# A third q/k operand set, first weights merged in PSUM, and a planner that picks one of two engines, in an LSH attention and feed-forward kernel

## The chip, the cores and the metric

The kernel runs on one core of a Trainium2 chip. The time is the device time of one execution in microseconds (us); the profile names the engines PE (TensorE matmul), PEld (its weight loads), DVE (VectorE), ACT (ScalarE), POOL (GpSimd) and SP (SyncE, which here only issues DMAs).

## What is computed

Attention in which a query sees only the keys of its own hash bucket, then two feed-forward layers one after the other, each with its own weights. All of it in float32 or better (the feed-forward weights come as float64).

```python
def _attn_ref(q, k, v, proj):            # (2, 8, 768, 64), proj (64, 6)
    q_bits = (q @ proj > 0); k_bits = (k @ proj > 0)
    mask = bucket(q_bits)[..., :, None] == bucket(k_bits)[..., None, :]
    scores = where(mask, q @ k.T / sqrt(D), -1e9)
    attn = exp(scores - max(scores)); attn /= sum(attn) + 1e-9
    return attn @ v
...
x = attn_out as (1536, 512)              # heads side by side
h = x @ w_in1;  x = (h * sigmoid(h)) @ w_out1      # w: 512x2048, 2048x512
h = x @ w_in2;  x = (h - tanh(h)) @ w_out2
```

## The kernel before

**Precision.** TensorE multiplies in a reduced float32 form, so every operand is split into a high part (a cast) and a low part (the value minus the cast), and a product is three matmuls: high by high, high by low, low by high. The casts and subtractions are most of the element-wise work.

**Attention.** There are 16 heads (8 of each batch) with 6 tiles of 128 queries by 768 keys. For a head, q and k come by DMA into a raw tile `r`; `q_hi` and `k_hi` (casts, ACT), `q_lo` and `k_lo` (subtractions, POOL; on DVE for head 0) make four operand tiles. `hash_mm` (L369) multiplies them with the projection, DVE turns signs into bits (L389 into `hb` and by DMA into the operands; L379 and L382 directly, for head 0). These bits make the scores of unlike buckets very small. A tile then goes: scores on PE (L503, four matmuls), the softmax read with the row maximum on DVE (L507), bias and exponent on ACT (L511, L514). After that a tile takes one of two ways. A *turned* tile (`direct`; every second one of batch 0, none of batch 1) is transposed by PE in two halves (L528), split into fp16 halves by ACT (L537) and DVE (L541). Any other is split by ACT (L556, `soft_hi`) and POOL (L559, `soft_lo`) and transposed by a DMA (L562) that SP issues. Both end in 18 small matmuls with V (L577 to L579). V is split too: row maxima (L422), a scale (L429 to L439), `v_hi` on ACT (L454), `v_lo` on DVE (L458). At a head's end DVE divides (L591 to L599); for every two heads PE transposes into x (L611), which is split into `xh` and `xl` (L616, L619).

**Feed-forward.** It works in groups of twelve matmuls of 128x384 (L828 for the hidden layer, L884 for the output), 256 groups in three passes: layer 1 of batch 0 (64 groups), layer 1 of batch 1 (64), layer 2 of both (128). Pass 0 needs x of batch 0 and fills TensorE between the tiles of batch 1; pass 1 needs x of batch 1. After a group of the hidden layer ACT takes a tanh (L832), DVE gates (L838 or L840), ACT casts (L843), DVE subtracts (L846).

**Weights.** They come as float64 words, in pieces of 128x512: absolute value (ACT, L755), clip (DVE, L758), shift (DVE, L762), sign (DVE, L766), merge with the low word (DVE, L770), cast (ACT, L774), subtraction (POOL, L778). The first eight pieces (`early`) keep the intermediate in the SBUF tile `wa`, later ones in a PSUM bank `cv`. The raw piece has two buffers, `wa` has two.

**Order.** A planner (`Plan.order`, L71 to L154) sets every engine's order when the program is built: each step has one engine, an estimated cost, a key (a due time, from `KNOBS`), what it depends on and which buffer slots it takes. Engine by engine it looks at the steps that could start, takes among those within `slack` of the earliest start the one with the smallest key, and books its buffers. On the chip each engine runs its own list strictly in order. Operand tiles of q and k have two sets of their own; for the first six heads the weight tiles `h0`, `l0` serve as a third. Raw q/k tiles have one slot and, for batch 0, two borrowed from `h1` and `l1`.

## Time and profile before

| | |
|---|---|
| median of 3 runs | 778.18 us (776.93 to 781.0) |
| profiled execution | 781.89 us |
| its span | 780.1 us |
| PE busy | 727.0 us (93%) |
| DVE busy | 561.7 us (72%) |
| ACT busy | 438.8 us (56%) |
| POOL busy | 309.6 us (40%) |

The span is the time from the first to the last instruction. The shares are means over quite different parts: until about 164 us the core does attention of batch 0 alone, until about 358 us attention of batch 1 with feed-forward groups between, and from there feed-forward alone, so the profile has to be read part by part. "PEclk" is TensorE's granted clock as a share of 2.4 GHz (0.5 is 1.2 GHz). Records of one engine overlap slightly, since an instruction's record begins before the end of the one ahead; where steps follow closely, the distance of their starts is what one costs.

### The profile page before, as it was taken

What the parts mean: (1) busy time and instruction counts of PE and PEld (TensorE: products, weight loads), DVE (VectorE), ACT (ScalarE), POOL (GpSimd) and SP (SyncE); (2) the same over time, 40 slices, a digit from 0 to 9 for tenths busy, and PEclk for the clock granted to TensorE, in tenths of its full rate; (3) what the DMA queues carried; (4) which work ended last, traced back from release to release, by engine and by line L of the source; (5) the groups of instructions that cost most, each with busy time, mean ns of one, the idle gap of its engine ahead of it and who ended that gap; (6) DMA issues with size and microseconds to landing.
All of it is one profiled execution on the core that took longest, in us unless ns stands there. A gap on an engine that the chain in (4) does not pass through costs nothing.

```text
span 780.1 us, 14311 instructions
## 1 busy us (share of the span) xinstructions
PE 727.0 (93%) x5492; PEld 700.2 (90%) x5492; DVE 561.7 (72%) x1029; ACT 438.8 (56%) x821; POOL 309.6 (40%) x214
## 2 busy tenths in 40 slices
PE   3679966789999998999999999999999999999998
PEld 1559855689899998999999999999999999999998
DVE  6888999788688987887735288998688467243342
ACT  3598987789589787776535244562533235022130
POOL 4166676447676777566644322211220022000000
PEclk9899989799999999999999999999999999999999
DMA  9576675659999999895234233324032020000102
GB/s 333 191 160 157 149 168 147 171 129 225 220 215 213 260 260 197 188 211 149 69 107 108 82 109 108 109 82 134 27 110 81 1 86 24 1 1 0 58 25 82
DMA packets 138879, 100.39 MB, mean 129 GB/s; under 512 B 115870, under 2 KB 118174, under 8 KB 138810
## 3 DMA queue, kind: packets, MB, share of 16 engines
q1 hardware_dynamic: 138522, 99.20, 50.7%
q8 instruction: 43, 0.70, 0.4%
q10 hardware_dynamic: 288, 0.28, 0.2%
q14 instruction: 26, 0.21, 0.1%
HBM read 57.95 MB, written 11.53 MB: 89 GB/s over the span
## 4 chain that ended last, share of the span: by engine, by line
PE 79%; DVE 7%; DMA 5%; ACT 4%; POOL 2%; issue 2%; SPq 0%; POOLq 0%; DVEq 0%; ACTq 0%
PE psm L884 34%; PE psm L828 33%; PE ps L503 6%; DMA pt<-hl 3%; PE pso L577 1%; ACT p L514 1%; PE pso L579 1%; PE pso L578 1%; DVE p L507 1%; PE psm L369 1%; DVE wa L766 1%; POOL hl L559 1%; ACT p L537 1%; PE psm L528 1%; POOL k L351 1%
## 5 line engine op out<-in xcount | busy, mean ns | idle before, releaser
L828 PE MATMUL psm<-xh,wh 128*128 128x384 f32 x512 | 173.0, 338 | 0.2 <-ACT x L626 0.2
L828 PE MATMUL psm<-xh,wl 128*128 128x384 f32 x512 | 172.3, 337 | 0.0
L828 PE MATMUL psm<-xl,wh 128*128 128x384 f32 x512 | 172.3, 337 | 0.0
L884 PE MATMUL psm<-gh,wh 128*128 128x384 f32 x512 | 171.9, 336 | 0.0
L884 PE MATMUL psm<-gh,wl 128*128 128x384 f32 x512 | 171.4, 335 | 0.0
L884 PE MATMUL psm<-gl,wh 128*128 128x384 f32 x512 | 171.3, 335 | 0.0
L559 POOL TENSOR_TENSOR hl<-p,hl 128x768 f16<-128x768 f32 x72 | 120.3, 1672 | 113.9 <-ACT hl L556 92.5
L778 POOL TENSOR_TENSOR wl<-wa,wh 128x512 fp32r<-128x512 f32 x64 | 83.0, 1303 | 178.6 <-ACT wh L774 156.9
L832 ACT ACTIVATE th<-psm 128x384 f32<-128x384 f32 x128 | 62.9, 491 | 108.4 <-PE psm L828 108.2
L507 DVE TENSOR_SCALAR_CACHE_REDUCE p<-ps 128x768 f32<-128x768 f32 x96 | 91.0, 953 | 17.3 <-PE ps L503 15.8
L891 DVE TENSOR_TENSOR acc<-acc,psm 128x384 f32<-128x384 f32 x96 | 52.7, 551 | 67.8 <-PE psm L884 67.3
L846 DVE TENSOR_TENSOR gl<-psm,gh 128x384 fp32r<-128x384 f32 x128 | 71.2, 556 | 36.3 <-ACT gh L843 36.1
L828 PEld LDWEIGHTS psm<-xh,wh 128*128 128x128 f32 x512 | 96.1, 188 | 0.5 <-ACT x L626 0.5
L884 PEld LDWEIGHTS psm<-gh,wh 128*128 128x128 f32 x512 | 96.4, 188 | 0.0
L884 PEld LDWEIGHTS psm<-gl,wh 128*128 128x128 f32 x512 | 96.4, 188 | 0.0
L884 PEld LDWEIGHTS psm<-gh,wl 128*128 128x128 f32 x512 | 96.2, 188 | 0.0
L828 PEld LDWEIGHTS psm<-xl,wh 128*128 128x128 f32 x512 | 96.2, 188 | 0.0
L828 PEld LDWEIGHTS psm<-xh,wl 128*128 128x128 f32 x512 | 96.1, 188 | 0.0
L503 PE MATMUL ps<-k,q 128*128 128x384 f32 x336 | 84.0, 379 | 11.6 <-DVE p L507 10.1
L514 ACT ACTIVATE p<-p,bi 128x768 f32<-128x768 f32 x96 | 89.6, 936 | 4.1
L843 ACT CAST gh<-psm 128x384 fp32r<-128x384 f32 x128 | 61.3, 479 | 48.4 <-DVE psm L840 35.5
L503 PEld LDWEIGHTS ps<-k,q 128*128 128x128 f32 x336 | 62.0, 208 | 15.8 <-DVE p L507 8.6
(95 smaller groups left out, 1241.7 us busy)
## 6 DMA issues: line engine op xcount, KB each, us to landing
w<-in_w_in_dram SPq DMA_DIRECT2D x32, 512.0 KB
w<-in_w_out_dram SPq DMA_DIRECT2D x32, 512.0 KB
r<-in_qkT_dram SPq DMA_DIRECT2D x15, 768.0 KB
wi<-wa SPq DMA_DIRECT2D x16, 256.0 KB
wo<-wa SPq DMA_DIRECT2D x16, 256.0 KB
w<-wi SPq DMA_DIRECT2D x16, 256.0 KB
w<-wo SPq DMA_DIRECT2D x16, 256.0 KB
vr<-in_v_dram SPq DMA_DIRECT2D x6, 512.0 KB
```

Of the source, the lines that this page charges most:

```text
L351: eng.tensor_tensor(k1, get(raw)[:, 1, :], k2.bitcast(F32), op=ALU.subtract)
L503: nc.tensor.matmul(out=get(ps)[:, u, 0:HS], lhsT=x[:, t * 128:(t + 1) * 128], rhs=c[:, u * HS:(u + 1) * HS], start=(j == 0), stop=(j == 1))
L507: nc.vector.tensor_scalar(get_p().rearrange("p (c s) -> p c s", c=2), get(ps)[:, :, 0:HS], FLOOR, None, op0=ALU.max, op1=ALU.max, accum_ou ...
L514: nc.scalar.activation(out=get_p(), in_=get_p(), func=ACTF.Exp, scale=0.125, bias=get(bi))
L559: nc.gpsimd.tensor_tensor(get_hl()[:, 1, :], get_p(), get_hl()[:, 0, :], op=ALU.subtract)
L778: nc.gpsimd.tensor_tensor(ll, get(wa).bitcast(F32), hh.bitcast(F32), op=ALU.subtract)
L828: nc.tensor.matmul(out=ps, lhsT=a[:, k, fs], rhs=b_[blk][:, k, :], start=(k == 0 and j == 0), stop=(k == KD - 1 and j == 2))
L832: nc.scalar.activation(out=get(th), in_=get(bk)[:, 0:NB], func=ACTF.Tanh, scale=0.5 if e == 0 else 1.0)
L843: nc.scalar.copy(g_tile(gh, "gh")[:, f, :], get(bk)[:, 0:NB])
L846: nc.vector.tensor_tensor(g_tile(gl, "gl")[:, f, :], get(bk)[:, 0:NB], g_tile(gh, "gh")[:, f, :].bitcast(F32), op=ALU.subtract)
L884: nc.tensor.matmul(out=ps, lhsT=a[:, f, ds], rhs=b_.tile[:, f, :], start=(f == 0 and j == 0), stop=(f == F - 1 and j == 2))
L891: nc.vector.tensor_tensor(acc_tile(), acc_tile(), get(bk)[:, 0:NB], op=ALU.add)
```

## The change

- *Operands.* `qk_slots` gets three sets of its own; the weight tiles `h0`, `l0` no longer serve as operands (`xsets=0`), and the raw slots borrowed from `h1`, `l1` serve five heads instead of eight. The freed SBUF comes from a smaller DMA scratch buffer.
- *Weights.* Absolute value and clip now work in `wa` for all pieces, and the clip may go to POOL. The shift writes from `wa` into a PSUM bank, borrowed from the matmul banks for the first eight pieces (`banks`) and `cv` for the others; sign works in the bank, and the merge reads it and writes `wa`.
- *Two engines.* Some steps (`q_hi`, `soft_hi`, the bias, the clip, the casts of x and of the gate among them) are given several engines. The planner lists such a step under each; one that isn't the first may take it only if start, cost and a bias `b_...` come out no later than on the first engine with what is queued there. A bias of 100 leaves the first engine alone.
- *Turned tiles.* The share is 0.4 in batch 0 (19 instead of 24) and 0.083 in batch 1 (4 instead of none).
- *Order.* Scores, softmax reads, fp16 halves, transposes and products with V are each taken in the order of the tiles (`line`). New keys: head 0 and the constants come first, V and the first weights later. Head 0's q and k are loaded ahead of head 1's. Two groups of the first hidden layer may run three quarters of their matmuls before the last quarter of x is there (`ahead`).

```diff
-KNOBS = dict(start=8.965, step=2.575, gap=10.136, step1=4.004, ffn=3.742, ffn3=2.182, pv=9, prep=14.527, hash=6.75,
-             slack=0.157, conv=22.093, conv0=74.277, vld=2.059, vmax=-3.882, vsplit=1.453, x2=0)
+KNOBS = dict(start=1.134, step=2.53, gap=9.343, step1=3.92, ffn=3.61, ffn3=2.222, pv=12.257, prep=16.11, hash=8.464,
...
+        def finish(t, e, at):
+            queue = sum(x.ways[e][0] for x in pend[e] if x is not t and x.key < t.key and len(x.ways) == 1)
+            return max(at, free[e] + queue) + t.ways[e][0]
+
...
+                    start = max(at, free[e])
+                    first = next(iter(t.ways))
+                    if e != first and start + t.ways[e][0] + t.bias > finish(t, first, at):
+                        continue
...
     qk_slots = [Slot(lambda i=i: tuple(qkp.tile([128, S], F32R, tag=f"{x}{i}", name=x) for x in ("q1", "q2", "k1", "k2")))
-                for i in range(2)]
+                for i in range(3)]
...
-        raw = Held(*(one(r_slots) + (r_extra if n < H else [])))
-        ops = Held(*(one(qk_slots) + ([(wtile["h0"], wtile["l0"])] if n < 6 else [])))
+        raw = Held(*(one(r_slots) + (r_extra if n < K["raws"] else [])))
+        ops = Held(*(one(qk_slots) + ([(wtile["h0"], wtile["l0"])] if n < K["xsets"] else [])))
...
-            direct = b == 0 and i % 2 == 1
+            share = K["direct"] if b == 0 else K["direct1"]
+            direct = int((i + 1) * share) > int(i * share)
...
-                th = add("ACT", 0.83, soft_hi, a + 1.5, [e], takes=[hl], uses=[p])
-                tl = add("POOL", 1.66, soft_lo, a + 2, [th], uses=[p, hl])
-                ready = [add("SP", 1.43, flip, a + 3, [tl], takes=[pt], uses=[hl], tail=1.5)]
+                th = add(("ACT", "POOL", "DVE"), (0.83, 1.66, 0.6), soft_hi, a + K["k_hi"], [e], takes=[hl], uses=[p], port=("DVE",), give="shi", line="hl")
+                tl = add(("POOL", "DVE"), (1.66, 0.95), soft_lo, a + K["k_lo"], [th], uses=[p, hl], port=("DVE",), give="slo")
+                ready = [add("SP", 1.43, flip, a + K["k_f"], [tl], takes=[pt], uses=[hl], tail=2.25, line="pt")]
...
-                        cvh = None if early else Held(*cvs)
...
+                        cvh = Held(*(banks if early else cvs))
...
+                            a = add("ACT", 0.65, c_abs, kj, [ld], takes=[wa], uses=[w])
+                            a = add(("POOL", "DVE"), (1.29, 0.42), c_clip, kj + 0.5, [a], uses=[wa], port=("DVE",), give="clip")
+                            a = add("DVE", 0.6, c_shift, kj + 1, [a] + gate_cv, takes=[cvh], uses=[wa])
+                            a = add("DVE", 0.69, c_sign, kj + 1.05, [a], uses=[cvh, w])
+                            a = add("DVE", 0.69, c_low, kj + 1.1, [a], uses=[cvh, w, wa])
...
-                        hm = add("PE", 2.08, h_mm, tk, wdone + xready[blk], takes=[bk], uses=[held])
+                        if ps_i == 0 and c == 0 and q * F + f < K["ahead"]:
+                            xr = xready[blk]
+                            hm = add("PE", 1.56, lambda h_mm=h_mm: h_mm(0, KD - 1), tk - K["by"], wdone + xr[:-2],
+                                     takes=[bk], uses=[held])
+                            hm = add("PE", 0.52, lambda h_mm=h_mm: h_mm(KD - 1, KD), tk, [hm] + xr[-2:], uses=[bk, held])
```

Three places show how the order moves. First DVE at the start of the program, before: `wa` is a weight piece, `vm` V's row maxima, `hb` the bits of head 1.

```order
L334 CAST q_176<-r 128x768
L343 TENSOR_TENSOR q_177<-r,q_176 128x768
L422 TENSOR_REDUCE vm<-vr 128x1 x2
L389 TENSOR_SCALAR hb<-psm,cst_sb 82x384 x2
L758 TENSOR_SCALAR wa<-wa 128x512
L762 TENSOR_SCALAR wa<-wa 128x512
L766 SCALAR_TENSOR_TENSOR wa<-w,wa 128x512
L770 SCALAR_TENSOR_TENSOR wa<-w,wa 128x512
L351 TENSOR_TENSOR k_178<-r,k_179 128x768
```

And now (L334, L385 and L392 are head 0's cast and subtractions, L424 and L427 its bits, L558 the softmax read):

```order
L334 CAST q_172<-r 128x768
L385 TENSOR_TENSOR q_173<-r,q_172 128x768
L392 TENSOR_TENSOR k_174<-r,k_175 128x768
L424 TENSOR_SCALAR q_173<-psm,cst_sb 18x384
L427 TENSOR_SCALAR k_175<-psm,cst_sb 18x384
L424 TENSOR_SCALAR q_173<-psm,cst_sb 18x384
L427 TENSOR_SCALAR k_175<-psm,cst_sb 18x384
L466 TENSOR_REDUCE vm<-vr 128x1
L558 TENSOR_SCALAR p,mx<-ps 128x768 x2
L434 TENSOR_SCALAR hb<-psm,cst_sb 82x384
```

Head 0's subtraction of k, which stood behind two V steps, head 1's bits and a whole weight piece, follows its other two steps at once, and two softmax reads stand where the weight piece stood; before, the first softmax read is row 33 of the list.

Second, DVE in the middle of batch 0 at one of the first weight pieces. Before, a piece is four steps in `wa`, as in the rows above. Now (L820 clip, L823 shift, L827 sign, L831 merge; `psm` is a borrowed bank):

```order
L820 TENSOR_SCALAR wa<-wa 128x512
L558 TENSOR_SCALAR p,mx<-ps 128x768
L823 TENSOR_SCALAR psm<-wa 128x512
L645 TENSOR_SCALAR den<-pso,vsc 128x6
L646 RECIPROCAL den<-den 128x6
L827 SCALAR_TENSOR_TENSOR psm<-w,psm 128x512
L595 TENSOR_TENSOR p<-psm,p 128x384
L831 SCALAR_TENSOR_TENSOR wa<-w,psm 128x512
```

The intermediate lies in the bank from the shift to the merge, and softmax and division steps stand between.

Third, PE where feed-forward work begins. Before (L503 scores, L611 transposes of x, L828 the hidden layer):

```order
L503 MATMUL ps<-k_2015,q_2013 128x384 x2
L503 MATMUL ps<-k_2016,q_2014 128x384 x2
L611 MATMUL psm<-cst_sb,xt 128x128 x6
L503 MATMUL ps<-k_2015,q_2013 128x384 x2
L503 MATMUL ps<-k_2016,q_2014 128x384 x2
L828 MATMUL psm<-xh_78,wh 128x384
L828 MATMUL psm<-xl_80,wh 128x384
L828 MATMUL psm<-xh_78,wl 128x384
```

Now (L554 scores, L892 the hidden layer; nine such rows stand here before a transpose of a turned tile follows):

```order
L554 MATMUL ps<-k_1377,q_1375 128x384 x2
L554 MATMUL ps<-k_1378,q_1376 128x384 x2
L892 MATMUL psm<-xh_78,wh 128x384
L892 MATMUL psm<-xl_80,wh 128x384
L892 MATMUL psm<-xh_78,wl 128x384
L892 MATMUL psm<-xh_78,wh 128x384
```

Before, the first hidden group stands behind the last transposes of x of batch 0; now nine matmuls of the first group, and two transposes of tiles later nine of the second, stand among the last head's tiles, ahead of those transposes of x.

## Rows read from the trace of the kernel before

**Rows 1.** Busy time by stretch: engine sums (instructions), granted clock, DMA share, GB/s.

```profile
core 0: us, PE busy (x) PEld busy (x) DVE busy (x) ACT busy (x) POOL busy (x), PEclk, DMA share, GB/s
0.00:31.00 31.00, 11.90 (x34) 8.48 (x34) 24.28 (x40) 10.80 (x15) 8.57 (x10) 0.99 0.84 300
31.00:90.00 59.00, 52.70 (x632) 46.20 (x633) 50.89 (x112) 52.63 (x102) 35.65 (x21) 0.95 0.65 143
90.00:164.40 74.40, 54.51 (x658) 47.04 (x657) 66.25 (x123) 60.73 (x113) 44.89 (x30) 0.89 0.67 166
164.40:357.60 193.20, 188.67 (x1763) 179.63 (x1762) 161.86 (x309) 154.42 (x277) 127.40 (x82) 0.99 0.99 215
357.60:780.00 422.40, 419.16 (x2411) 418.84 (x2409) 258.44 (x447) 160.19 (x317) 93.14 (x73) 1.00 0.22 68
```

**Rows 2.** Chain that ended last (start, us, what): the first feed-forward groups.

```profile
164.36 6.36 PE psm L828 x36
```

**Rows 3.** Waits of PE from 31 to 164 us: total, times, longest.

```profile
PE ps L503 <- DVE p L507: 12.1, 9, 5.0
```

**Rows 4.** Instructions in order of time (start, us, engine, line), start of the program.

```profile
5.88 0.38 DVE L303 CAST hw<-x 128x410 fp32r<-128x410 f32 x1 [5.01 <-DMA x<-in_proj_dram]
7.24 2.02 DVE L334 CAST q<-r 128x768 fp32r<-128x768 f32 x1 [0.36 <-DMA r<-in_qkT_dram]
9.30 2.44 DVE L343 TENSOR_TENSOR q<-r,q 128x768 fp32r<-128x768 f32 x1
...
17.32 0.95 DVE L351 TENSOR_TENSOR k<-r,k 128x768 fp32r<-128x768 f32 x1
...
21.68 1.63 PE L503 MATMUL ps<-k,q 128*128 128x384 f32 x4
23.10 0.52 PE L369 MATMUL psm<-q,hw 128*82 128x384 f32 x1
...
28.26 0.61 DVE L382 TENSOR_SCALAR k<-psm,cst_sb 18x384 fp32r<-18x384 f32 x1
...
31.02 0.96 DVE L507 TENSOR_SCALAR_CACHE_REDUCE p<-ps 128x768 f32<-128x768 f32 x1
```

**Rows 5.** Groups by line and form, whole span: busy us, mean ns, idle before.

```profile
L758 DVE TENSOR_SCALAR cv<-cv 128x512 f32<-128x512 f32 x56 | 38.9, 694 | 6.5 <-ACT cv L755 6.4
L762 DVE TENSOR_SCALAR cv<-cv 128x512 int32<-128x512 int32 x56 | 38.9, 694 | 0.8
L766 DVE SCALAR_TENSOR_TENSOR cv<-w,cv 128x512 int32<-128x512 int32 x56 | 38.7, 691 | 0.7
...
L766 DVE SCALAR_TENSOR_TENSOR wa<-w,wa 128x512 int32<-128x512 int32 x8 | 9.5, 1184 | 0.2
L770 DVE SCALAR_TENSOR_TENSOR wa<-w,wa 128x512 int32<-128x512 int32 x8 | 8.2, 1019 | 0.2
L758 DVE TENSOR_SCALAR wa<-wa 128x512 f32<-128x512 f32 x8 | 5.9, 735 | 0.0
L762 DVE TENSOR_SCALAR wa<-wa 128x512 int32<-128x512 int32 x8 | 4.1, 517 | 0.2
```

**Rows 6.** Instructions in order of time: transposes, halves, and the first gating step.

```profile
85.22 0.87 PE L528 MATMUL psm<-cst_sb,p 128*128 128x128 f32 x6
...
112.86 1.01 DVE L541 TENSOR_TENSOR p<-psm,p 128x384 f16<-128x384 f32 x2
...
164.78 2.73 DVE L458 SCALAR_TENSOR_TENSOR v16l<-vr,vsc,v 128x512 f16<-128x512 f32 x4
167.45 0.56 DVE L838 SCALAR_TENSOR_TENSOR psm<-th,psm 128x384 f32<-128x384 f32 x1
```

**Rows 7.** Instructions in order of time, POOL and DVE, around a first weight piece.

```profile
105.03 1.64 POOL L559 TENSOR_TENSOR hl<-p,hl 128x768 f16<-128x768 f32 x1 [0.75 <-DVE wa L762]
105.06 2.16 DVE L766 SCALAR_TENSOR_TENSOR wa<-w,wa 128x512 int32<-128x512 int32 x1
...
122.99 1.28 POOL L778 TENSOR_TENSOR wl<-wa,wh 128x512 fp32r<-128x512 f32 x1 [3.29 <-ACT wh L774]
```

**Rows 8.** Waits of SP's queue from 31 to 164 us: total, times, longest.

```profile
SPq L562 <- POOL hl L559: 41.1, 15, 5.5
...
SPq L731 <- DVE wa L770: 2.9, 1, 2.9
```

More of the change, by code (lines that the diff above doesn't have):

```diff
@@ L353, in lsh_attention_moe_kernel @@
[L353 to L358 removed]
+            ENG[e].tensor_tensor(q2[lo, :], get(raw)[lo, 0, :], q1[lo, :].bitcast(F32), op=ALU.subtract)
```

314 lines of the change are left out of this document (179 added, 135 removed).

## The prediction

> **What bounds the kernel now.** I read the stretches first [rows 1]. From 357.6 us to the end TensorE is busy 419.2 of 422.4 us at full clock; what is missing is the last output on its way to memory. Nothing that the change does on other engines can shorten that stretch. From 164.4 to 357.6 us it is busy 188.7 of 193.2 us: attention of batch 1 with feed-forward groups between (twelve matmuls of 128x384, 2.1 us each, [rows 2]), which could as well stand later at the same rate. So the time is the moment at which feed-forward work begins to fill TensorE (164.4 us, [rows 2]), plus a nearly fixed amount of TensorE work, plus the tail. Before that moment TensorE has 119.1 us of work in 164.4, in part at half clock (granted 0.95 and 0.89 on average, [rows 1]); its longest wait there is for VectorE's softmax reads, L507, 12.1 us [rows 3]. VectorE is busy 24.3 + 50.9 + 66.3 = 141.4 us of it. ScalarE is close behind: 52.6 of 59 us between 31 and 90 [rows 1].
>
> Two things inside that first part are dear. The first softmax read starts only at 31.0 us [rows 4]: head 0's data is ordered behind head 1's, and two weight pieces and the whole V preparation stand ahead of it on VectorE, whose cast and subtraction of head 0 take 2.0 and 2.4 us while GpSimd works on another head; the next subtraction of that size (L351) takes 0.95. And the first eight weight pieces, whose intermediate lies in SBUF (wa), pay 1.18 us for the sign step L766 and 1.02 for the merge L770, where the later ones, in PSUM (cv), pay 0.69 [rows 5].
>
> **Anchor.** The profiled execution took 781.9 us (span 780.1). The median of the runs, 778.2, is 3.7 lower; I work out a difference on the profiled span and subtract it from 778.2. My mark is the first gating step L838 at 167.45 us [rows 6], since the order shows which VectorE instructions stand ahead of it in both kernels.
>
> **The change, term by term, on VectorE up to the mark.** Busy before: 141.4 plus the four V splits between (2.7, [rows 6]) = 144.1; idle so 23.3.
> - Sign step in a borrowed bank: 8 x (1.184 - 0.691) = -3.9. Merge: 8 x 1.019 = 8.2 becomes 7 x 0.69 = 4.8 (the eighth stands behind the mark): -3.4 [rows 5].
> - Clip: nine (8 x 0.735 + 0.69 = 6.6) become three (2.2), five go to GpSimd: -4.4 [rows 5].
> - Shift, now from SBUF into PSUM, a form that is not in the trace: the nearest rows are 0.517 (SBUF) and 0.694 (PSUM) [rows 5]; I take the dearer, 8 x 0.694 against 8 x 0.517 + 0.69: +0.7 (from -0.7 to +0.7).
> - Fewer turned tiles: 19 instead of 24 in batch 0, and one of batch 1 ahead of the mark, so 40 steps L541 instead of 48; two in a row take 1.01 us [rows 6]: 8 x 0.505 = -4.0.
> - Head 0 with no other head's subtraction on GpSimd beside it: at most 2.02 + 2.44 - 0.6 - 0.95 = -2.9, at least 0; I take -2.5, nearest to the 0.95 row [rows 4].
> - V splits 10 to 7: 3 x 0.7 = -2.1, merely later. Three more batch-1 softmax reads at 0.95, of which 0.07 overlaps: +2.6. One cast to fp16 moved onto VectorE: +0.6, an estimate from the shift rows.
>
> Sum: -3.9 - 3.4 - 4.4 + 0.7 - 4.0 - 2.5 - 2.1 + 2.6 + 0.6 = -16.4, so 127.7 us.
>
> **When the stage starts.** The first data still comes at 5.9 us [rows 4]. Casting the constants (0.95), then cast and two subtractions of head 0 (0.6 + 0.95 + 0.95) lead to 9.4; from the first hash matmul to the end of the last bit step 5.8 (23.10 to 28.87), first scores 1.6: the first softmax read stands at about 16.8 instead of 31.0 [rows 4]. That is no gain of 14.2 us by itself, since the V and weight work that stood there is done later. Of the 127.7 us, 6.6 lie ahead of 16.8; 121.1 follow. From 31 to 164.4 VectorE was busy 117.1 of 133.4 us, 0.878. At the same density 121.1 / 0.878 = 137.9, and the mark falls at 154.7: **12.8 us earlier**.
>
> Does ScalarE allow that density? Its work up to the mark was 124.2 [rows 1] + 2.7. Changes: eight casts of turned halves -3.4, five fp16 casts +4.2, three pairs of bias and exponent +3.4, one q cast +0.8, V, weight and abs steps that come later -3.1: 128.8. Some 5.9 lie ahead of 16.8, so 122.9 in 137.9 us, 0.89. From 31 to 90 us the pair ran at 0.86 and 0.89 [rows 1]: this is the densest that the trace has shown, and no more.
>
> **Behind the mark.** Two feed-forward groups run three quarters of their matmuls ahead, in gaps. The first is complete before the mark in either kernel; the second's nine matmuls save 1.6. Four turned tiles in batch 1 add 8 x 0.43 = 3.5 us of TensorE work (six transposes take 0.87, [rows 6]); three more scores (0.7 each) and one more hash (1.05) done early take 3.2 off. The 4.5 us of idle between 164.4 and 357.6 I leave. Sum: -12.8 - 1.6 + 0.3 = -14.1. I forecast 778.2 - 14.1 = **764 us**.
>
> **Cover.** The clips on GpSimd (5 x 1.3, from a piece's subtraction, [rows 7]) and five more softmax subtractions (5 x 1.64, [rows 7]) bring it from 89 to 104 busy us, two thirds of the stage: hidden, as long as no transpose waits for them. Five more DMA transposes and their issue go through SyncE's queue, which waited 41.1 us for GpSimd's halves from 31 to 164 us [rows 8] and so has room. The third operand set adds no work. At the end of attention the order leaves 4 feed-forward groups (8.4 us) behind the last transposes of x, where 9 stood before; x needs two copies, a cast and four subtractions, some 0.9 + 0.5 + 4 x 1.3 = 6.6 us. If this cover fails, the price is 1 to 4 us.
>
> **A rule against the change.** At 105.06 us L766 took 2.16 us; GpSimd's L559 ran from 105.03 to 106.67 [rows 7]: VectorE stood until it ended. The Trainium skill (Perfetto Trace Analysis, Optimizing Scalar/DVE Operations) says that moving work between VectorE and GpSimd might not help, since they share an SBUF port. By it, the sign and merge steps would not come down, and what leaves VectorE as clips would come back as waits. The rows speak for the saving: the sign steps on cv average 0.69 although GpSimd was busy 127 of 193 us where many of them stand [rows 1, 5]. As a rival it stands below.
>
> **Rivals.**
> 1. *The pair of VectorE and ScalarE does not reach 0.88 and 0.89* with weights, V and tiles overlapping from the start; at 0.83 the mark falls at 16.8 + 145.9 = 162.7, a gain of 4.8 + 1.6 - 0.3: 772. For it: ScalarE reached 0.89 in one stretch of 59 us only.
> 2. *GpSimd blocks VectorE as before*: 3.9 + 3.4 = 7.3 us more work, / 0.878 = 8.3 us of the gain gone: 772.
> 3. *Denser than before*: a third operand set, and steps that may go to the engine that is free, take waits away (TensorE's 12.1 us, [rows 3]); at 0.92 the mark falls at 148.4, gain 20.4, or 25 with the idle 4.5 us: 753 to 758.
> 4. *No change*: the early start is eaten whole, feed-forward still begins near 164: 776 to 780.
> 5. *Slower*: SyncE's queue is in order. A raw piece is freed only by its merge step, which may now stand behind a clip on GpSimd, behind softmax subtractions; the next piece's load then blocks the transposes behind it, the products with V starve, and the score buffers fill. Such waits for L770 cost 2.9 us from 31 to 164 [rows 8]. Point of decision: if each of six loads holds the queue 2.4 us longer with nothing to cover it, the 14.1 us are gone; at 4 us each the time is 788.
>
> **Chances.** Forecast (759 to 768) 0.54; rival 1 0.16; rival 2 0.05; rival 3 0.12; rival 4 0.07; rival 5 0.06. A measurement of this kernel can tell about 0.5% (3.9 us) from no change. Faster 0.87, same 0.07, slower 0.06. The range from 753 to 774 holds the forecast, rivals 1 and 2 and most of 3.
>
> **What would show it.** First softmax read at 15 to 18 us; sign and merge rows near 0.69; VectorE's busy time up to the first gate near 128 us and that gate near 155; TensorE idle from there to the end of attention under 8 us; the stretch after attention unchanged. The forecast is wrong if the early start does not carry to the first gate, if sign steps still average over 1 us, or if SyncE's waits for weight pieces pass 15 us in the first part.

## The result, and the profile after

The kernel after takes 754.34 us (median of 4 runs, 753.97 to 756.73), the kernel before, on the same chip, 777.84 (776.93 to 781.0): a ratio of 0.970, interval 0.966 to 0.973. The gain is 23.5 us where 14.1 were forecast. The two profiled executions, 781.89 and 754.19 us, are 27.7 apart, since the one of before lies 4 us above its median (more on this below).

Stretches of the kernel after, cut at its first softmax read, its first gating step and near the end of attention (columns as in [rows 1]):

```profile
0.00:12.75 12.75, 4.80 (x15) 3.52 (x16) 6.53 (x12) 5.76 (x7) 4.75 (x9) 1.00 0.87 326
12.75:147.53 134.78, 112.28 (x1322) 98.33 (x1322) 120.04 (x255) 121.64 (x228) 101.42 (x64) 0.94 0.93 207
147.53:340.00 192.47, 191.87 (x1802) 183.80 (x1801) 167.34 (x317) 149.49 (x272) 147.42 (x92) 1.00 0.93 213
340.00:752.00 412.00, 409.05 (x2353) 408.73 (x2351) 237.66 (x420) 153.16 (x308) 116.71 (x83) 1.00 0.22 67
```

The same of the kernel before, cut at its own first gating step:

```profile
31.00:167.45 136.45, 110.27 (x1305) 96.30 (x1306) 120.19 (x240) 116.41 (x220) 80.94 (x50) 0.92 0.67 157
167.45:357.60 190.15, 185.62 (x1746) 176.58 (x1745) 158.81 (x305) 151.37 (x271) 127.00 (x81) 0.99 0.99 216
```

The first gating step comes at 147.53 us instead of 167.45 [rows 6]: 19.9 of the 27.8 us between the spans. The other 7.9 lie behind it (span less gate: 612.65 before, 604.77 after). Over half of that is TensorE's idle time: up to the end of attention it was idle 190.15 - 185.62 = 4.5 us, and is idle 192.47 - 191.87 = 0.6; in the last stretch 3.2 became 3.0. The idle time of before has one main cause, late transposes. Its waits from 167.45 to 357.6 us (total, times, longest), the longest of them in order of time, and the stretch right behind it (columns as in [rows 1]):

```profile
PE pso L577 <- DMA pt<-hl: 4.2, 4, 2.5
```

```profile
310.01 0.20 PE L577 MATMUL pso<-v,pt 128*128 128x65 f16 x1 [2.48 <-DMA pt<-hl]
```

```profile
310.10:313.50 3.40, 3.40 (x26) 3.40 (x27) 1.78 (x4) 0.00 (x0) 0.75 (x1) 0.50 1.09 234
```

TensorE stood idle for 2.48 us, and for the 3.4 us behind that its granted clock was 0.50 (1.2 GHz). Matmuls of 128x384 start 0.32 us apart in it and 0.17 us apart at full clock, so about half of it is lost, an estimate of 1.7 us. That is part of the 3.9 us by which TensorE's busy time behind the gate fell (604.78 to 600.92); the kernel after has no such stretch there. The other 2.2 us are in part matmul work that now stands ahead of the gate. The groups behind it, by line and form, first before, then after:

```profile
L828 PE MATMUL psm<-xh,wh 128*128 128x384 f32 x506 | 170.9, 338 | 0.2 <-ACT x L626 0.2
...
L503 PE MATMUL ps<-k,q 128*128 128x384 f32 x176 | 41.2, 356 | 0.1
```

```profile
L892 PE MATMUL psm<-xh,wh 128*128 128x384 f32 x502 | 169.5, 338 | 0.0
...
L554 PE MATMUL ps<-k,q 128*128 128x384 f32 x168 | 38.3, 349 | 0.6 <-DVE p L558 0.6
```

Much of the 4.2 us of waits and of the 1.7 us at the lower clock need not come back in every execution of before. The profile of e7_nosign (below) has the same 4155 matmuls in the order of before behind its gate; its waits for transposes there are 1.4 us, no stretch there is at half clock, and the stretch is 4.15 us shorter, 608.50 instead of 612.65:

```profile
160.70:769.20 608.50, 603.26 (x4155) 593.81 (x4153) 416.90 (x751) 311.54 (x587) 220.22 (x154) 1.00 0.46 115
```

So up to some 4 of the 7.9 us seem to go with the execution that was profiled, which fits its 4 us above the median, and not with the kernel. The split is not exact: the profile of e7_nosign is one execution too, 3 us below its own median.

The start in order of time (columns as in [rows 4]):

```profile
4.71 0.38 DVE L346 CAST hw<-x 128x410 fp32r<-128x410 f32 x1 [3.85 <-DMA x<-in_proj_dram]
...
5.62 0.55 DVE L334 CAST q<-r 128x768 fp32r<-128x768 f32 x1
...
6.20 0.96 DVE L385 TENSOR_TENSOR q<-r,q 128x768 fp32r<-128x768 f32 x1
...
6.22 0.61 PE L414 MATMUL psm<-q,hw 128*82 128x384 f32 x1 [6.22 <-DVE q L334]
7.08 0.95 DVE L392 TENSOR_TENSOR k<-r,k 128x768 fp32r<-128x768 f32 x1
...
11.39 0.61 DVE L427 TENSOR_SCALAR k<-psm,cst_sb 18x384 fp32r<-18x384 f32 x1
...
12.75 0.96 DVE L558 TENSOR_SCALAR_CACHE_REDUCE p<-ps 128x768 f32<-128x768 f32 x1
```

Head 0 is cast in 0.55 us and its two subtractions take 0.96 and 0.95; the cast took 2.02 and the first subtraction 2.44 before [rows 4]. The first hash matmul runs right behind the cast, at 6.22, and the last bits of head 0 are done at 12.00. The first softmax read starts at 12.75 us instead of 31.02.

Groups of VectorE and GpSimd by line and form (busy us, mean ns, idle before), the steps of a weight piece:

```profile
L823 DVE TENSOR_SCALAR psm<-wa 128x512 int32<-128x512 int32 x8 | 5.5, 686 | 0.1
L827 DVE SCALAR_TENSOR_TENSOR psm<-w,psm 128x512 int32<-128x512 int32 x8 | 5.5, 685 | 0.0
L831 DVE SCALAR_TENSOR_TENSOR wa<-w,psm 128x512 int32<-128x512 int32 x8 | 5.4, 670 | 0.0
...
L820 DVE TENSOR_SCALAR wa<-wa 128x512 f32<-128x512 f32 x31 | 24.0, 776 | 8.8 <-ACT wa L817 8.4
```

```profile
L839 POOL TENSOR_TENSOR wl<-wa,wh 128x512 fp32r<-128x512 f32 x64 | 83.2, 1302 | 107.9 <-ACT wh L835 107.5
L820 POOL TENSOR_SCALAR wa<-wa 128x512 f32<-128x512 f32 x33 | 63.7, 1931 | 43.9 <-ACT wa L817 43.7
```

In the borrowed banks the early shift, sign and merge steps take 0.686, 0.685 and 0.670 us, where sign and merge took 1.184 and 1.019 in SBUF [rows 5]. A clip on GpSimd takes 1.93 us.

What TensorE waited for from 12.75 to 147.53 us, and what SyncE's queue waited for there (total, times, longest):

```profile
PE pso L631 <- DMA pt<-hl: 5.6, 5, 3.1
PE ps L554 <- DVE p L558: 3.4, 4, 1.2
```

```profile
SPq L616 <- POOL hl L613: 33.0, 17, 6.5
...
SPq L785 <- DVE wa L831: 0.7, 1, 0.7
```

The wait for softmax reads fell from 12.1 us [rows 3] to 3.4 us. SyncE waits 33.0 us for GpSimd's halves where it waited 41.1, and 0.7 for the merge of a weight piece where it waited 2.9 [rows 8].

### The profile page after: what moved, and what is told of

The parts are those of the page before. It is cut to its first block, busy times and chain, and to the rows that moved or that the text cites. A ratio compares the mean times of both kernels' runs of the same rounds, so it can differ in the third digit from the quotient of the medians.

```text
span 752.3 us, 14254 instructions
## 1 busy us (share of the span) xinstructions
PE 718.0 (95%) x5486; PEld 694.4 (92%) x5486; DVE 531.6 (71%) x1002; ACT 430.0 (57%) x813; POOL 370.3 (49%) x247
## 4 chain that ended last, share of the span: by engine, by line
PE 66%; DVE 1%; ACT 0%; issue 0%; ACTq 0%; DVEq 0%
PE psm L954 32%; PE psm L892 30%; PE ps L554 2%; PE pso L631 1%; PE pso L632 1%; PE pso L633 1%; DVE p L558 0%; PE psm L414 0%; PE psm L665 0%; DVE wa L820 0%; DVE wa L831 0%; DVE acc L961 0%; ACT p L568 0%; DVE p L595 0%; DVE cv L827 0%
## 5 line engine op out<-in xcount | busy, mean ns | idle before, releaser
L892 PE MATMUL psm<-xh,wh 128*128 128x384 f32 x512 | 173.2, 338 | 0.7 <-ACT xh L334 0.4
L892 PE MATMUL psm<-xl,wh 128*128 128x384 f32 x512 | 172.4, 337 | 0.2 <-DVE xl L673 0.2
L892 PE MATMUL psm<-xh,wl 128*128 128x384 f32 x512 | 172.4, 337 | 0.0
L839 POOL TENSOR_TENSOR wl<-wa,wh 128x512 fp32r<-128x512 f32 x64 | 83.2, 1302 | 107.9 <-ACT wh L835 107.5
L558 DVE TENSOR_SCALAR_CACHE_REDUCE p<-ps 128x768 f32<-128x768 f32 x96 | 90.2, 951 | 14.7 <-PE ps L554 8.3
L892 PEld LDWEIGHTS psm<-xh,wh 128*128 128x128 f32 x512 | 96.1, 188 | 1.5 <-DVE p L595 0.9
L892 PEld LDWEIGHTS psm<-xl,wh 128*128 128x128 f32 x512 | 96.2, 188 | 0.4 <-DVE xl L673 0.4
L892 PEld LDWEIGHTS psm<-xh,wl 128*128 128x128 f32 x512 | 96.1, 188 | 0.0
L554 PE MATMUL ps<-k,q 128*128 128x384 f32 x384 | 90.2, 362 | 5.0 <-DVE p L558 4.0
L334 ACT CAST gh<-psm 128x384 fp32r<-128x384 f32 x124 | 59.4, 481 | 50.5 <-DVE psm L904 36.2
L820 POOL TENSOR_SCALAR wa<-wa 128x512 f32<-128x512 f32 x33 | 63.7, 1931 | 43.9 <-ACT wa L817 43.7
```

What stands on the lines that cost most here:

```text
L334: nc.scalar.copy(out, in_) if e == "ACT" else ENG[e].tensor_copy(out, in_)
L554: nc.tensor.matmul(out=get(ps)[:, u, 0:HS], lhsT=x[:, t * 128:(t + 1) * 128], rhs=c[:, u * HS:(u + 1) * HS], start=(j == 0), stop=(j == 1))
L558: nc.vector.tensor_scalar(get_p().rearrange("p (c s) -> p c s", c=2), get(ps)[:, :, 0:HS], FLOOR, None, op0=ALU.max, op1=ALU.max, accum_ou ...
L820: ENG[e].tensor_scalar(lead(), lead(), W_MIN, W_MAX, op0=ALU.max, op1=ALU.min)
L839: ENG[e].tensor_tensor(ll, get(wa).bitcast(F32), hh.bitcast(F32), op=ALU.subtract)
L892: nc.tensor.matmul(out=ps, lhsT=a[:, k, fs], rhs=b_[blk][:, k, :], start=(k == 0 and j == 0), stop=(k == KD - 1 and j == 2))
```

## Theories and experiments

By the **load theory** (the prediction's) the time of the first gating step goes by the element-wise work that VectorE and ScalarE have up to it. By the **order theory** it goes by the order in detail: the planner's numbers (its table KNOBS and the keys) were set for exactly this form of the kernel, any other order of the same work is worse, and the parts themselves matter little. All kernels were timed in turn with the kernel before, which had medians of 777.3, 778.1 and 778.3 us in the three batches; the kernel after was timed in a batch of its own, so a difference to it is between batches, and the ratios are the safer measure. "Gate" is the start of the first gating step in the profiled execution, "rest" its span less the gate, "VectorE" its busy time between the first softmax read and the gate, with the share of that stretch, and "clock" TensorE's granted clock there.

| kernel | median us (range) | ratio to before, interval | gate us | rest us | VectorE us (share) | clock |
|---|---|---|---|---|---|---|
| before | 777.84 (776.9 to 781.0) | | 167.45 | 612.65 | 120.2 (0.88) | 0.92 |
| after | 754.34 (754.0 to 756.7) | 0.970, 0.966 to 0.973 | 147.53 | 604.77 | 120.0 (0.89) | 0.94 |
| order of after: e1_sbuf | 762.03 (761.8 to 764.6) | 0.981, 0.977 to 0.984 | 154.66 | 605.24 | 127.8 (0.90) | 0.94 |
| order of after: e2_dupdve | 757.22 (755.6 to 760.6) | 0.974, 0.970 to 0.979 | 155.21 | 603.49 | 124.0 (0.87) | 0.93 |
| order of after: e3_dupact | 757.91 (756.9 to 759.5) | 0.974, 0.970 to 0.979 | 153.23 | 603.77 | 119.2 (0.85) | 0.94 |
| order of before: e7_nosign | 773.84 (771.0 to 776.9) | 0.993, 0.990 to 0.996 | 160.70 | 608.50 | 111.4 (0.86) | 0.94 |
| laid out anew: e4_slack | 766.54 (766.0 to 768.5) | 0.986, 0.982 to 0.990 | 152.8 | 612.1 | 122.1 (0.87) | 0.91 |
| laid out anew: e5_oldkeys | 770.31 (768.8 to 772.0) | 0.990, 0.987 to 0.993 | 157.3 | 611.2 | 114.0 (0.85) | 0.94 |
| laid out anew: e6_oldparts | 776.45 (772.4 to 778.0) | 0.998, 0.995 to 1.001 | 159.7 | 613.8 | 131.5 (0.89) | 0.90 |
| laid out anew: e8_sets | 776.17 (771.1 to 778.7) | 0.998, 0.995 to 1.001 | 157.5 | 618.5 | 115.9 (0.80) | 0.86 |
| laid out anew: e9_sets2 | 770.41 (768.3 to 772.9) | 0.991, 0.987 to 0.994 | 152.8 | 613.7 | 116.2 (0.83) | 0.88 |
| laid out anew: e10_bslack | 782.71 (779.6 to 784.1) | 1.005, 1.003 to 1.007 | 169.7 | 611.4 | 120.1 (0.87) | 0.89 |
| laid out anew: e11_one | 770.96 (770.5 to 771.6) | 0.991, 0.988 to 0.994 | 158.3 | 610.5 | 123.2 (0.85) | 0.88 |
| laid out anew: e12_turn | 768.79 (765.5 to 769.2) | 0.989, 0.985 to 0.992 | 156.0 | 607.7 | 125.9 (0.88) | 0.92 |

Neither theory fits all of these rows. The load theory alone would put the gates of e8_sets and e9_sets2 ahead of that of the kernel after, since they have 4 us less of VectorE's work and 6 us less of ScalarE's behind the same first read; they come 10.0 and 5.3 us later, since VectorE is busy only 0.80 and 0.83 of the stretch:

```profile
12.90:157.50 144.60, 114.50 (x1297) 100.76 (x1297) 115.87 (x242) 115.71 (x215) 103.42 (x65) 0.86 0.76 181
```

So the amount of work is one factor, and how densely it gets done in an order is another (in these two the missing set may have a part in it, see below). TensorE's granted clock up to the gate is 0.86 to 0.94 in the kernels that were laid out anew and 0.93 or 0.94 in those with the order of after; whether that delays the gate or only follows from TensorE's waits, no run here separates.

### The same order, one cost changed

**The borrowed bank taken back.** The instructions stand in the order of the kernel after on every engine; only the memory of the early intermediate is SBUF again.

```diff
-                        def mid(cvh=cvh):
-                            return get(cvh).bitcast(I32)
+                        def mid(cvh=cvh, wa=wa, early=early):
+                            return (get(wa) if early else get(cvh)).bitcast(I32)
```

> The changed kernel in the same order on every engine, but the first eight weight pieces keep their intermediate in the SBUF tile wa instead of the borrowed PSUM bank. If VectorE's work ahead of the first gate sets the time (load theory): sign and merge go back from 0.69 and 0.67 to 1.1 us or more while GpSimd is busy, shift falls from 0.69 to about 0.5, so 8 x 0.45 + 8 x 0.35 - 8 x 0.15 = 5 to 8 us more, first gate at 152 to 156, 759 to 763 us. If the gain is the early start and the order alone, and the work has slack (order theory): 754 to 756 us.

It took 762.03 us, 7.7 more than the kernel after (8.5 by the ratios), within the load theory's range. Groups by line and form, and the stretch up to the gate:

```profile
L831 DVE SCALAR_TENSOR_TENSOR wa<-w,wa 128x512 int32<-128x512 int32 x8 | 11.3, 1416 | 0.0
L827 DVE SCALAR_TENSOR_TENSOR wa<-w,wa 128x512 int32<-128x512 int32 x8 | 10.2, 1280 | 0.0
L823 DVE TENSOR_SCALAR wa<-wa 128x512 int32<-128x512 int32 x8 | 5.9, 738 | 0.0
```

```profile
12.75:154.66 141.91, 114.04 (x1326) 100.33 (x1325) 127.81 (x257) 122.46 (x228) 105.49 (x64) 0.94 0.88 197
154.66:759.90 605.24, 600.93 (x4151) 591.98 (x4150) 406.98 (x736) 302.42 (x579) 264.38 (x175) 1.00 0.45 114
```

The three steps cost 27.4 us in all instead of 16.4. VectorE is busy 127.8 us instead of 120.0 behind the first softmax read and up to the gate, the gate falls 7.1 us later, and the rest is the same. So the bank is worth 7.7 us, near the 8.3 at which rival 2 priced its loss. The instructions of one form, one line for each kernel (min/median/max ns, first and last start), show why. First with the early intermediate in SBUF, then of the kernel after:

```profile
L827 DVE SCALAR_TENSOR_TENSOR wa<-w,wa x8: 673/1260/2036, 46.1 to 154.1; 128x512 int32<-128x512 int32 x8
```

```profile
L827 DVE SCALAR_TENSOR_TENSOR psm<-w,psm x8: 676/685/695, 45.5 to 146.9; 128x512 int32<-128x512 int32 x8
```

With both inputs in SBUF the same step takes from 0.67 to 2.04 us; with one in PSUM it never takes over 0.70, although GpSimd was busy 101.4 of 134.8 us. Two of the steps in SBUF, and what GpSimd did beside them:

```profile
112.94 1.84 POOL L613 TENSOR_TENSOR hl<-p,hl 128x768 f16<-128x768 f32 x1
113.55 1.78 DVE L827 SCALAR_TENSOR_TENSOR wa<-w,wa 128x512 int32<-128x512 int32 x1
...
126.92 2.09 POOL L820 TENSOR_SCALAR wa<-wa 128x512 f32<-128x512 f32 x1
127.75 0.67 DVE L827 SCALAR_TENSOR_TENSOR wa<-w,wa 128x512 int32<-128x512 int32 x1
```

The first starts while GpSimd subtracts and ends at 115.33 us, 0.55 after the subtraction's end at 114.78. All 11 sign and merge steps in SBUF that took over 0.7 us are of this kind, and each ends 0.55 us after the subtraction that was running when it started. The other five of the 16 took 0.67 to 0.68: one had nothing beside it, beside two the subtraction began after them, and two started during a clip of GpSimd. The Trainium skill (SBUF — State Buffer, SBUF: two separate sides) says that VectorE and GpSimd lock a shared pair of ports for a whole instruction, VectorE's operations with two SBUF inputs among them. The 11 long steps agree with it, and so does the kernel after, where one input lies in PSUM. The two steps beside a clip, 0.67 and 0.68 us, do not show it: there the lock went with GpSimd's two-input subtractions, not with its one-input clip, so the clips that moved to GpSimd did not come back as waits of these steps.

**VectorE's and ScalarE's work added.** In the first kernel the early sign step runs twice (8 x 0.685 = 5.5 us of VectorE), in the second the early absolute value (5.4 us of ScalarE).

```diff
-                            nc.vector.scalar_tensor_tensor(mid(), w_tile()[:, :, 1], -0x40000000, mid(), op0=ALU.bitwise_and,
-                                                           op1=ALU.bitwise_or)
+                            for _ in range(2 if early else 1):
+                                nc.vector.scalar_tensor_tensor(mid(), w_tile()[:, :, 1], -0x40000000, mid(), op0=ALU.bitwise_and,
+                                                               op1=ALU.bitwise_or)
```

> The changed kernel in the same order, with the sign step of the first eight pieces done twice on VectorE (the second time changes nothing): 8 x 0.69 = 5.5 us more VectorE work ahead of the first gate. Load theory: first gate at 152 to 154, 759 to 761 us. Order theory: the idle 14.7 us in that stage take it up, 754 to 756.

```diff
-                            nc.scalar.activation(out=lead(), in_=w_tile()[:, :, 1].bitcast(F32), func=ACTF.Abs)
+                            for _ in range(2 if early else 1):
+                                nc.scalar.activation(out=lead(), in_=w_tile()[:, :, 1].bitcast(F32), func=ACTF.Abs)
```

> The changed kernel in the same order, with the absolute value of the first eight pieces done twice on ScalarE: 8 x 0.67 = 5.4 us more ScalarE work ahead of the first gate. If VectorE alone sets the stage: 0 to 2 us, 754 to 756. If VectorE and ScalarE set it as a pair, each busy 0.89 to 0.90 of it: 3 to 6 us, 757 to 760.

They took 757.22 us (+2.9) and 757.91 (+3.6). The first lies between the ranges of both theories, the second in that of the pair. A microsecond of VectorE's work ahead of the gate costs 2.9 / 5.5 = 0.5 us, one of ScalarE's 3.6 / 5.4 = 0.7 (by the ratios both took 3.6 more, 0.7 each). That fits two engines that bound the first part together, and not one alone. Whether GpSimd, busy 0.75 of the stretch, has a price too was not tried. The prices are rough, since the runs of each kernel spread over 3 to 5 us and those of the first overlap with those of the kernel after. (The profile of the first is of its slowest run, 760.6 us, so its gate is late.) The stretch up to the gate with ScalarE's work added:

```profile
12.50:153.23 140.73, 112.58 (x1324) 98.01 (x1322) 119.22 (x257) 126.92 (x236) 101.92 (x64) 0.94 0.92 198
```

**Work taken out of the kernel before**, in its own order: without the early sign step.

```diff
-                        def c_sign(w_tile=w_tile, t_of=t_of):
+                        def c_sign(w_tile=w_tile, t_of=t_of, early=early):
                             u = t_of().bitcast(I32)
+                            if early:
+                                return
```

> The kernel before in its own order with the sign step of the first eight weight pieces left out (these weights lose their sign): 8 x 1.18 = 9.5 us less VectorE work ahead of the first gate. In the changed kernel 5.5 us more cost 2.9 and 11 us more cost 7.7, 0.5 to 0.7 of the work. Load theory: 5 to 9 us less, 768 to 773. Order theory: under 3 us, 774 to 778.

It took 773.84 us against 778.13: 4.3 less by the medians, 5.4 by the ratio, for 8 x 1.184 = 9.5 us of work [rows 5]: again about 0.5 us for a microsecond. By the median that is just short of the load theory's range, by the ratio inside it. In the profile, which is of its fastest run, the gate falls at 160.70, 6.8 earlier, and VectorE is busy 8.8 us less behind the first softmax read than before (120.2):

```profile
31.00:160.70 129.70, 110.30 (x1305) 96.03 (x1306) 111.37 (x233) 116.20 (x220) 78.99 (x50) 0.94 0.76 165
```

### The order laid out anew

**One number of the planner.** The kernel after with slack 0.05 instead of 0.042, nothing else.

```diff
-              slack=0.042, conv=33.419, conv0=52.708, vld=10.124, vmax=13.049, vsplit=16.427, x2=0.271, direct=0.4,
+              slack=0.05, conv=33.419, conv0=52.708, vld=10.124, vmax=13.049, vsplit=16.427, x2=0.271, direct=0.4,
```

> The changed kernel with the planner's slack at 0.05 instead of 0.042: same work, another order in detail. A measure of how much a re-planned order moves the time by itself. Load theory: within 3 us of the changed kernel, 751 to 758. Order theory (the tuned order is the gain): 5 to 15 us slower, 759 to 770.

It took 766.54 us, 12.2 more, with the same instructions but for a few element-wise steps that changed engine. The gate falls 5.3 us later, and the rest is 7.3 longer:

```profile
12.80:152.80 140.00, 115.85 (x1323) 101.68 (x1323) 122.06 (x255) 124.87 (x233) 104.60 (x64) 0.91 0.88 205
152.80:764.90 612.10, 603.56 (x4153) 592.30 (x4151) 405.57 (x738) 299.63 (x574) 262.50 (x174) 1.00 0.43 111
```

Behind the gate TensorE is idle 612.10 - 603.56 = 8.5 us, where the kernel after has 3.9. The two longest of its waits there are for steps that stand late on VectorE (total, times, longest):

```profile
PE psm L892 <- DVE gl L910: 1.6, 1, 1.6
PE psm L892 <- DVE xl L732: 1.2, 1, 1.2
```

That is the order theory's range (759 to 770), and the load theory's (751 to 758) missed. Some of it is load, since the planner moved steps between engines: VectorE has 2.0 us more work up to the gate, ScalarE 3.2. But most of the 12 us hangs on the order in detail, which the load theory doesn't see.

**The old keys, the old parts.** Two kernels to part the two: the new parts under the old numbers and start keys (what a part that did not exist before needs, it keeps), and the old parts under the new ones. In the second the clip is back on VectorE, no group runs ahead and the sets are the old ones as well; absolute value and clip still work in `wa`, and the rule `line` stays, so it is not quite the old form.

```diff
-KNOBS = dict(start=1.134, step=2.53, gap=9.343, step1=3.92, ffn=3.61, ffn3=2.222, pv=12.257, prep=16.11, hash=8.464,
-             slack=0.042, conv=33.419, conv0=52.708, vld=10.124, vmax=13.049, vsplit=16.427, x2=0.271, direct=0.4,
+KNOBS = dict(start=8.965, step=2.575, gap=10.136, step1=4.004, ffn=3.742, ffn3=2.182, pv=9, prep=14.527, hash=6.75,
+             slack=0.157, conv=22.093, conv0=74.277, vld=2.059, vmax=-3.882, vsplit=1.453, x2=0, direct=0.4,
...
-    hash_ready = add("DVE", 1.0, prep_hash, -55, [c_proj])
+    hash_ready = add("DVE", 1.0, prep_hash, 0, [c_proj])
...
-        at = a0 - K["prep"] if n else -50.0
+        at = a0 - K["prep"] if n else 0.0
```

> The changed kernel with the numbers of the kernel before in every knob that both have (start, step, prep, hash, conv0, the V keys, slack and the like), the old offsets of the softmax steps, and head 0 no longer first. All parts stay: third operand set, bank merge, two-engine choice, share 0.4, two groups ahead. Load theory (the 16.4 us less VectorE work carry the gain): 757 to 763 us, first softmax read again near 25 to 31 us. Order theory (the new keys carry it): 768 to 780.

```diff
-             slack=0.042, conv=33.419, conv0=52.708, vld=10.124, vmax=13.049, vsplit=16.427, x2=0.271, direct=0.4,
-             direct1=0.083, b_qh=1.32, b_qlo=100, b_kup=100, b_vlo=2, b_bi=2.75, b_thi=100, b_shi=0.98, b_slo=100,
+             slack=0.042, conv=33.419, conv0=52.708, vld=10.124, vmax=13.049, vsplit=16.427, x2=0.271, direct=0.5,
+             direct1=0.0, b_qh=100, b_qlo=100, b_kup=100, b_vlo=100, b_bi=100, b_thi=100, b_shi=100, b_slo=100,
...
-                for i in range(3)]
+                for i in range(2)]
...
-                            return get(cvh).bitcast(I32)
+                            return (get(wa) if early else get(cvh)).bitcast(I32)
```

> The reverse: the new keys and head 0 first, but every part taken back: two operand sets and the weight tiles as a third, first weights in SBUF, each step on one engine and the clip on VectorE, every second tile of batch 0 turned and none of batch 1, no group ahead. Load theory: most of the gain goes, 769 to 780 us. Order theory: 756 to 766.

They took 770.31 and 776.45 us. The stretches up to the gate, first the old keys, then the old parts:

```profile
22.60:157.30 134.70, 109.27 (x1292) 94.62 (x1291) 113.99 (x239) 115.94 (x218) 100.21 (x62) 0.94 0.86 188
157.30:768.50 611.20, 604.66 (x4165) 593.77 (x4163) 402.12 (x732) 306.92 (x581) 278.37 (x183) 1.00 0.45 112
```

```profile
12.80:159.70 146.90, 117.05 (x1328) 104.02 (x1327) 131.46 (x260) 118.43 (x226) 81.95 (x50) 0.90 0.74 170
159.70:773.50 613.80, 603.47 (x4153) 593.19 (x4151) 412.68 (x758) 312.88 (x588) 226.19 (x156) 1.00 0.46 116
```

With the old keys the first softmax read starts at 22.6 us, and VectorE has less to do up to the gate (15.7 + 114.0 = 129.7 us), but is busy only 0.85 of the stretch. With the old parts it starts at 12.8 us and VectorE is busy 0.89, but with 131.5 us of work behind that start instead of 120.0. Either brings the gate to 157 to 160, some 8 to 10 us earlier than before; both together brought 19.9. For the gate the two nearly add up. Behind it neither brings more than 1.5 of the 7.9 us, and in time they are far from adding up: 7.8 and 1.7 us by the medians, against 23.5 together. The ranges do not decide either: the first lies in the order theory's (768 to 780), the second in the load theory's (769 to 780).

**Two operand sets, twice.** The third set is the old borrowed one again (with the buffers for raw pieces as they were), under two values of slack.

```diff
-              xsets=0, raws=5, vmax1=70.287, emode=1, lmode=1)
+              xsets=6, raws=8, vmax1=70.287, emode=1, lmode=1)
...
-                for i in range(3)]
+                for i in range(2)]
```

> The changed kernel with two operand sets of its own and the weight tiles h0, l0 as a third for the first six heads again, raw slots for eight heads as before; all else as changed, the order planned anew. By the load theory the third set adds no work and saves none: 754 to 760 us, no more than a re-planned order moves. If the set itself takes waits away (rival 3): 762 to 775, with TensorE waiting for hash operands.

> The kernel after with two own operand sets of q and k and the old borrowed third, as in the run before this one, but with the planner's slack at 0.05 instead of 0.042, so that it lays out another order. Set theory: the borrowed third set itself costs (its memory becomes free only when the stage has gone through, and a wait of 5.4 us on the copies of a head's hash bits was seen with it), so another order does not bring it back: 766 to 778 us, and a wait of several us of the score matmuls on an operand is there again. Order theory: the 22 us above 754 were mostly the luck of one order, a second order lands anywhere between 757 and 770 us and the wait on the operand is gone.

The first took 776.17 us, above both ranges, and by itself reads as a price of 22 us for the set. The second, with slack 0.05, took 770.41, inside the set theory's range and just above the order theory's. TensorE's longest single wait is the same in both (waits up to about the gate, first e8_sets, then e9_sets2):

```profile
PE ps L554 <- DMA k<-hb: 5.4, 1, 5.4
```

```profile
PE ps L554 <- DMA k<-hb: 5.3, 1, 5.3
```

That wait was to be the mark of the missing set. But the kernel with the old shares of turned tiles (below), which has three own sets, shows it as well:

```profile
PE ps L554 <- DMA k<-hb: 4.7, 1, 4.7
```

So it is no such mark. With slack 0.05 three sets took 766.54 us and two 770.41, a difference of 3.9; with slack 0.042 the three sets have the order that was set for them, and the two sets a strange one. What an own third set is worth these runs don't settle.

**The kernel before, laid out anew**, to see what another order costs a kernel whose parts are untouched.

```diff
-             slack=0.157, conv=22.093, conv0=74.277, vld=2.059, vmax=-3.882, vsplit=1.453, x2=0)
+             slack=0.05, conv=22.093, conv0=74.277, vld=2.059, vmax=-3.882, vsplit=1.453, x2=0)
```

> The kernel before, its parts untouched, with the planner's slack at 0.05 instead of 0.157: nothing but another order of the same work. Order theory (an order in detail is worth some 10 us either way, and a table of numbers that was set for one form gives a worse order on any other): 782 to 800 us. Load theory (the time goes by the element-wise work up to the first gate, which is the same here but for about one more block of early weights, 2 to 5 us): 775 to 783 us.

It took 782.71 us, 4.4 more than the kernel before, and its gate, 169.7, is 2.3 later. That lies in both ranges (782 to 800 by the order theory, 775 to 783 by the load theory), so it decides nothing between them; as a price of another order it is a third of the 12 us above.

**One engine for each step, and the old shares of turned tiles.**

```diff
-              direct1=0.083, b_qh=1.32, b_qlo=100, b_kup=100, b_vlo=2, b_bi=2.75, b_thi=100, b_shi=0.98, b_slo=100,
-              b_xh=1.72, b_xlo=1.56, b_wlo=100, b_clip=-0.24, b_hhi=0.67, k_m=-0.273, k_e=0.107, k_t=1.899,
+              direct1=0.083, b_qh=100, b_qlo=100, b_kup=100, b_vlo=100, b_bi=100, b_thi=100, b_shi=100, b_slo=100,
+              b_xh=100, b_xlo=100, b_wlo=100, b_clip=100, b_hhi=100, k_m=-0.273, k_e=0.107, k_t=1.899,
...
-                            a = add(("POOL", "DVE"), (1.29, 0.42), c_clip, kj + 0.5, [a], uses=[wa], port=("DVE",), give="clip")
+                            a = add(("DVE", "POOL"), (0.42, 1.29), c_clip, kj + 0.5, [a], uses=[wa], port=("DVE",), give="clip")
```

> The kernel after without the choice between two engines: each element-wise step has its one engine as before the change (the clip on VectorE, the copies of evictions on ScalarE), the third set, the borrowed banks, the fewer turned tiles and the numbers of the planner stay; the order is laid out anew. Up to the first gate VectorE gets about 6 clips, one shift, one sign and one merge more (about 6 us) and 3 softmax readings less (3 us). Load theory: by half a microsecond for each of these 3 us, and without the 1.9 us clips on GpSimd, 754 to 759 us. Order theory: the order is another one, 760 to 772 us, as in the run that changed the slack alone. If the choice of engine itself carries the gain: over 765 us with VectorE as the engine that the matmuls wait for after the first gate too.

```diff
-              slack=0.042, conv=33.419, conv0=52.708, vld=10.124, vmax=13.049, vsplit=16.427, x2=0.271, direct=0.4,
-              direct1=0.083, b_qh=1.32, b_qlo=100, b_kup=100, b_vlo=2, b_bi=2.75, b_thi=100, b_shi=0.98, b_slo=100,
+              slack=0.042, conv=33.419, conv0=52.708, vld=10.124, vmax=13.049, vsplit=16.427, x2=0.271, direct=0.5,
+              direct1=0.0, b_qh=1.32, b_qlo=100, b_kup=100, b_vlo=2, b_bi=2.75, b_thi=100, b_shi=0.98, b_slo=100,
```

> The kernel after with the old shares of turned tiles (0.5 of the probability tiles of the first pass by way of TensorE, none in the second, instead of 0.4 and 0.083); the order is laid out anew. VectorE gets 8 turned-tile splits more before the first gate (0.95 us each, 7.6 us) and TensorE their transposes. Load theory: 757 to 762 us, at half a microsecond for each microsecond of VectorE before the gate. Order theory: 760 to 772 us, no better told from the run that changed the slack alone. If the turned tiles were worth nothing: 753 to 756 us.

They took 770.96 and 768.79 us, both in the order theory's ranges and above the load theory's. Both are 2 to 4 us above the kernel whose slack alone was changed, so neither part can be told from the order: whether it is worth anything beyond that is open. With the choice of engine gone, TensorE's waits from 150 us on name DMA for 1.5 us, VectorE's softmax reads for 1.3 and nothing else above 0.4 us, so VectorE didn't become the main thing that the matmuls wait for there.

## Why the prediction was right, and where it was mis-sized

The forecast was faster, 764 us, with a range of 753 to 774; it came out 754.3, within the range but at its lower end, at the edge of rival 3 (753 to 758). The main step was as forecast: the gate comes earlier because VectorE has less to do and begins sooner, and the runs in the same order (e1 to e3, e7) show that this work has a price. Two things were not. The rest behind the gate is not nearly fixed: it is 603.5 to 618.5 us in the profiles above. And the forecast has no term for how well an order fits, which e4_slack shows to be worth up to 12 us; with the same parts and that other order the kernel takes 766.5 us, 2.5 from the forecast. The terms:

- **Work up to the gate: right.** Forecast 127.7 us, measured 6.5 + 120.0 = 126.6. Single terms were off and cancelled: the steps of head 0 fell further than the 2.5 us taken, to 0.55 + 0.96 + 0.95 (the bound of 2.9 was reached), and the three clips left on VectorE took 2.7 us, not 2.2. On GpSimd a clip costs 1.93 us, not the 1.3 of a subtraction; that was covered: GpSimd was busy 101.4 of 134.8 us, and SyncE's waits for its halves fell.
- **Start of the stage: off by 4.1 us.** Forecast 16.8, measured 12.75. The forecast had both subtractions of head 0 ahead of the first hash matmul, at 9.4; it needs only the cast, and ran at 6.22: 1.9 us by that and 1.2 because the first data came at 4.71 instead of 5.88 [rows 4]. From there to the last bits it took 5.8 us as forecast, and from the bits to the softmax read 0.75 instead of 1.6.
- **Density: nearly right.** Forecast 0.878, measured 120.04 / 134.78 = 0.891 on VectorE and 121.64 / 134.78 = 0.903 on ScalarE, against 0.89 forecast. Worth 1.9 us; the rival's 0.92 was not reached. Start 4.1, work 1.2 (1.06 / 0.878) and density 1.9 make the 7.2 us by which the gate came before the forecast 154.7, most of the 9.4 us by which the gain was too small.
- **Idle time behind the gate: left alone without a reason, and it went.** "The 4.5 us of idle between 164.4 and 357.6 I leave": 3.9 of it went. That is rival 3's last clause. Of the 4.5 us, 4.2 were waits for late transposes, the longest of which the 3.4 us at half clock followed. In the profile of e7_nosign, in the order of before, these waits are 1.4 us, so a part of the 3.9 may be the execution and not the kernel. What is left goes with the order: in the four kernels with the order of after the rest is 603.5 to 605.2 us, in every other one 607.7 to 618.5, with the new parts as without them. (A profile is one run, and those of before and e7_nosign are 4 us above and 3 below their medians, so the lower end of the second range lies near the first.)
- **Busy time behind the mark: -1.3 forecast, -3.9 measured.** 1.7 of it is the 3.4 us at half clock in the profile of before, which no term foresaw. In place of nine, some twelve first-layer products less stand behind the mark (three forms as L892, four fewer of each); the eight fewer score matmuls are two tiles, not three, and the hash matmuls are as many as before (36), not a head's fewer; of the forecast's 24 new transposes there are 18. At the forecast's own prices these counts make -2.1 - 1.4 + 2.6 = -0.9, so some 1.3 us stay unexplained.
- **Rival 2 and the rule behind it.** By it 772 us; the steps in the borrowed banks took 0.67 to 0.69, so it didn't come; e1_sbuf shows that without the banks it would have, by way of GpSimd's subtractions and not of the clips.
- **Rival 5.** SyncE's queue waited 0.7 us for a weight piece; the cover at the end of attention held too, with 0.6 us of idle up to 340 us.
- **The third set and the planner's choice, priced at nothing:** not settled, as told above.

How the gain splits can be said in part. The bank is worth 7.7 us (same order, one change). With slack 0.05 in both, the new kernel against the old one is 782.71 - 766.54 = 16.2 us (14.6 by the ratios); the numbers that were set for each make it 23.5. So about two thirds of the gain came with the parts and the early start under an order that was not set for them, and some 7 to 9 us came from an order that fits. That is one draw of the order on either side, and another would move the split. Why the order of after has none of the late transposes behind its gate was not traced to single instructions.

## What to carry to other kernels

Find the moment at which the main engine gets work without end, and price a change by the element-wise work ahead of that moment: here one microsecond of it on one engine was worth 0.5 to 0.7, not 1, which fits two engines that share the bound. Where a planner's numbers are set for one form of a kernel, compare parts in the same order of instructions; a new order alone moved the time by 4 to 12 us, where the one part that could be priced was worth 7.7. Where two profiles are compared, look for what only one execution may have had: here up to 4 of 27.7 us. And keep one operand of a two-input VectorE step in PSUM where GpSimd subtracts beside it.

## What was not expected of the hardware

- A clip (two-scalar max and min, 128x512 fp32) takes 1.93 us on GpSimd, a subtraction of two tensors of that size 1.30 (L839): the step with one input is the slower one there, and not by waiting, since its shortest is 1.91.
- The shift from SBUF into PSUM takes 0.686 us, like the one from PSUM to PSUM (0.694 [rows 5]), not the 0.517 of SBUF to SBUF.
- The same sign step in SBUF averaged 1.28 us in one order (e1_sbuf) and 0.98 in another (e6_oldparts). In the first six of eight took over 0.8 us, in the second two, and all of these ended 0.55 us after a GpSimd subtraction: what GpSimd costs VectorE depends on what happens to stand beside it. Two such steps beside a GpSimd clip took no longer than alone.
